# A decode step with attention and a feed-forward layer: the first piece of w2 is loaded as 112 rows, its last 16 rows by eight small transfers placed among wo's pieces

## The chip, the cores and the metric

The kernel runs on one core of a Trainium2 chip. The metric is the device time of one execution in microseconds (us); lower is better. Differences of about 0.2% (0.7 us) are what is looked at here.

## The reference

One token (batch 1, one query position, width 512) goes through a block whose layer norms are modulated by a condition `c`. Attention has 32 query heads on 8 key/value heads of size 128, over a cache of 32768 positions; the feed-forward layer is 512 to 1792 to 512 with a ReLU. All inputs are bfloat16.

```python
mod = silu(c) @ w_mod                      # six vectors of 512: sa, ca, ga, sb, cb, gb
h = layernorm(x) * (1 + ca) + sa
q = h @ wq                                 # 32 heads of 128
p = softmax(q @ k_cache.T * 128**-0.5)     # 4 query heads share one of 8 kv heads
x = x + ga * ((p @ v_cache) @ wo)          # wo: 4096 x 512
h = layernorm(x) * (1 + cb) + sb
x = x + gb * (relu(h @ w1) @ w2)           # w1: 512 x 1792, w2: 1792 x 512
```

The two caches are 64 MB each, so nearly all of the time is the reading of about 149 MB from HBM.

## The kernel before

**One stream of loads.** Everything large is loaded by SP (the SyncE queue) through one helper, `stream_dma` (line 141), in the order of the list `stream`: a half of K of head 0, `w_mod`, `wq`, the rest of K of head 0, then K of head g+1 and V of head g in turn, at the end V of the last head in three pieces, then the four pieces of `wo` (`WOP`: 4, 2, 1 and 1 kv heads, that is 2048, 1024, 512 and 512 KB), the two pieces of `w1` (`W1P`: 1344 and 448 KB) and the six pieces of `w2` (`W2P`: 512, 384, 384, 256, 128 and 128 KB). `need(key)` issues the list up to the key that is wanted; `load(key)` works out the tile and the source of one entry. Every one of these transfers has 128 rows, one for each partition of SBUF.

**Where they go.** Three slots of 64 KB per partition form a ring; `wo`, `w1` and `w2` share one slot, the tile `tail_sb`. The first transfer into it waits until the slot's earlier user, a K tile, has been read.

**Completion.** Each transfer adds to one of eight completion semaphores, taken in turn. A transfer that takes a semaphore waits, on SP, until the transfer eight before it has landed. For the last transfers of the list that means: `w1`'s second piece waits for the first V piece of the last head, `w2`'s first and second piece for the second and third; `w2`'s pieces three to six wait for `wo`'s four pieces.

**The end.** After the last head TensorE (PE) projects with `wo` (`project`, line 582 for the first three pieces, 588 for the last), VectorE (DVE) and ScalarE (ACT) do the second layer norm, PE does `w1` (line 744), the hidden row is transposed and put through the ReLU (lines 754 and 755), and PE works through `w2` piece by piece (line 767, four matmuls for each of 14 column blocks: 16, 12, 12, 8, 4 and 4 matmuls for the six pieces), each piece as soon as it has landed. Two DVE operations (lines 772 and 774) and the store of 1 KB (line 775) follow.

Of the kernel before, what the change touches and what calls it, by code (L numbers as in the profile page):

```python
# [17 lines left out]
def kernel(  # L18
# [28 lines left out]
    WOP = [(0, Hkv // 2), (Hkv // 2, Hkv // 4), (Hkv - 2, 1), (Hkv - 1, 1)]  # L47
    WOROWS = 3
    LAST = Hkv - 1
# [3 lines left out]
    W1P = [(0, KT - 1), (KT - 1, KT)]  # L53

    OUT0, OUT1 = 30, 34
    assert Dh == 128 and REP == 4 and D == 512 and FT == W2P[-1][1] and NTILE == 4
    scale = float(Dh) ** -0.5
    eps = 1e-5
# [8 lines left out]
    def wo_v(i):  # L67
        g0, n = WOP[i]
        return A_wo[g0 * REP * Dh:(g0 + n) * REP * Dh, :].rearrange("(p r) d -> p r d", p=P)
# [19 lines left out]
    loaded, last_loop, end_b = {}, [], []  # L89
# [12 lines left out]
    def piece(name, at, n):  # L102

        if name not in pieces:
            pieces[name] = ring.tile([P, NTILE * TK * Dh], BF16, tag="slot", name=name)
        return pieces[name][:, at:at + n]

    def load(key):
        kind = key[0]
        if kind == "wm":  # L110
            t = piece("wmq_sb", 0, WM).rearrange("p (kt n) -> p kt n", kt=KT)
            src = wm_v
        elif kind == "wq":
            t = piece("wmq_sb", WM, WQ).rearrange("p (kt n) -> p kt n", kt=KT)
            src = wq_v
        elif kind in "kv":
            g, steps = key[1], key[2]
            src = (kv if kind == "k" else vv)[g, :, TK * steps[0]:TK * (steps[-1] + 1), :]
            name = f"Ksb{g}" if kind == "k" else f"Vsb{g}"
            t = piece(name, TK * Dh * steps[0], TK * Dh * len(steps)).rearrange("p (j d) -> p j d", d=Dh)  # L120
        elif kind == "wo":
            g0, n = WOP[key[1]]
            t = piece("tail_sb", g0 * REP * D, n * REP * D).rearrange("p (r d) -> p r d", d=D)
            src = wo_v(key[1])
        elif kind == "w1":
            k0, k1 = W1P[key[1]]
            t = piece("tail_sb", WO + k0 * Dff, (k1 - k0) * Dff).rearrange("p (kt f) -> p kt f", f=Dff)
            src = w1_v[:, k0:k1]
        else:
            f0, f1 = W2P[key[1]]  # L130
            t = piece("tail_sb", WO + KT * Dff + f0 * D, (f1 - f0) * D).rearrange("p (f d) -> p f d", d=D)
            src = w2_v[:, f0:f1]
        stream_dma(t, src)
        if kind in "kv":
            for i, u in enumerate(steps):
                loaded[(kind, g, u)] = t[:, TK * i:TK * (i + 1), :]
        else:
            loaded[key] = t

    def stream_dma(dst, src):  # L140
        i = nc.sync.dma_start(out=dst, in_=src)  # L141
        tc.stamp_issue_order_token(i.ins, "sp_stream")
        if last_loop:

            tc.add_manual_dep(i.ins, last_loop[0], mybir.DependencyInfo(
                mybir.DependencyClass.NoSync, mybir.DependencyReason.DATA))

    whole, halves = [(0, 1, 2, 3)], [(0, 1), (2, 3)]
    stream = [("k", 0, halves[0]), ("wm",), ("wq",), ("k", 0, halves[1])]
    for g in range(LOOPED):  # L150
        stream += [("k", g + 1, s) for s in (halves if g >= HALVED else whole)] + [("v", g, s) for s in (halves if g >= HALVED else whole)]
    for s in halves:
        stream += [("k", LAST, s), ("v", LOOPED, s)]
    stream += [("v", LAST, (0, 1)), ("v", LAST, (2,)), ("v", LAST, (3,))] + [("wo", i) for i in range(len(WOP))]
    stream += [("w1", i) for i in range(len(W1P))] + [("w2", i) for i in range(len(W2P))]
    pos = [0]

    def need(key):
        while key not in loaded:
            load(stream[pos[0]])  # L160
            pos[0] += 1
        return loaded[key]
# [19 lines left out]
    for hp in range(4):  # L182
        h, par = hp // 2, hp % 2
        src = AP(ib.tensor, ib.offset + 64 * h + par, [[ib.ap[0][0], P], [0, 4], [2, 32]])
# [130 lines left out]
    for u in range(2):  # L315
        for half in range(2):
            t = need(("k", 0, u))[:, 32 * half:32 * half + 32, :].rearrange("p j d -> p (j d)").bitcast(F32)
# [488 lines left out]
```

## Time and profile before

| what | value |
|---|---|
| median of 3 runs | 354.75 us (354.69 to 354.9) |
| the profiled execution | 354.43 us |
| its span, from the first to the last instruction | 352.5 us |
| HBM read | 149.42 MB, 424 GB/s over the span |
| PE busy | 276.4 us (78%) |
| DVE busy | 200.9 us (57%) |

The profiled execution takes 1.93 us more than its span. Busy shares say little here: the 16 DMA engines are busy nearly all the time, and which wait ends last in the final 15 us is what an edit of the last loads touches. In a row of the windows view stand the window, its length, the busy time of each engine with its instructions, the granted TensorE clock, the mean busy share of the 16 DMA engines and the GB/s that they moved.

### The profile page before, as it was taken

The numbers are of one execution on the slowest core, as the hardware profiler recorded it, in microseconds if no ns is written. First come the engines' busy times: TensorE is split into PE (matmuls) and PEld (weight loads), VectorE is DVE, ScalarE is ACT, GpSimd is POOL, SyncE is SP. The second block draws the span as 40 slices with busy tenths as digits, with TensorE's granted clock in tenths as the row PEclk, the third lists the DMA queues.
The fourth block names the chain that finished last, engine by engine and source line by source line (L and its number), as shares of the span: only waits on it lengthen the run. The fifth ranks groups of instructions, "written<-read, shape, count | busy, mean of one in ns | idle before, by whom it ended". The sixth has DMA issues, their size and how long they took to land. (4 is left out here: it accounts for less than half of the span.)

```text
span 352.5 us, 3650 instructions
## 1 busy us (share of the span) xinstructions
PE 276.4 (78%) x1285; PEld 112.7 (32%) x1285; DVE 200.9 (57%) x226; ACT 25.1 (7%) x69; POOL 3.1 (1%) x15
## 2 busy tenths in 40 slices
PE   0055891995998599976998499867999789989976
PEld 0021330341333233422433233322444334434433
DVE  6662464984079613974099506975684357744142
ACT  1200103002000200001000200011000100011000
POOL 2000000000000000000000000000000000000000
PEclk9996897698999969996999989996999999999986
DMA  8999989989999999899899899999999999999995
GB/s 353 404 436 440 496 372 469 461 379 469 431 409 455 424 424 461 387 448 469 387 454 469 387 455 461 396 402 450 435 422 424 450 429 420 433 454 403 429 413 217
DMA packets 5379, 149.58 MB, mean 424 GB/s; under 512 B 632, under 2 KB 888, under 8 KB 1784
## 3 DMA queue, kind: packets, MB, share of 16 engines
q1 hardware_dynamic: 5336, 149.43, 98.5%
q8 instruction: 8, 0.13, 0.1%
q14 instruction: 3, 0.02, 0.0%
q10 hardware_dynamic: 32, 0.00, 0.0%
HBM read 149.42 MB, written 0.00 MB: 424 GB/s over the span
## 5 line engine op out<-in xcount | busy, mean ns | idle before, releaser
L426 DVE STREAM_TRANSPOSE Ksb<-Ksb 128x2048 f32<-128x2048 f32 x60 | 133.1, 2275 | 59.6 <-DMA Ksb<-in_A_k_cache_dram 59.6
L507 PE MATMUL o_ps<-Vsb,P_g 128*16 (+1 forms) x512 | 126.6, 405 | 13.3 <-ACT P_g L482 10.0
L445 PE MATMUL S_ps<-Ksb,qbd 128*128 128x512 bf16 x512 | 120.8, 388 | 10.4 <-DVE Ksb L426 8.7
L445 PEld LDWEIGHTS <-qbd 128*128 128x128 bf16 x512 | 49.8, 99 | 77.7 <-issue 21.8
L507 PEld LDWEIGHTS o_ps<-Vsb,P_g 128*16 x352 | 33.6, 95 | 68.2 <-issue 38.3
L507 PEld LDWEIGHTS <-P_g 128*16 128x16 bf16 x160 | 13.8, 90 | 19.0 <-issue 0.4
L407 ACT COPY qbd<-qrep_sb 32x16 bf16<-32x16 bf16 x32 | 6.4, 201 | 175.2 <-PE S_ps L445 174.0
L487 DVE STREAM_TRANSPOSE P_g<-P_g 128x1024 bf16<-128x1024 bf16 x8 | 10.0, 1245 | 14.1 <-ACT P_g L482 14.1
L458 DVE TENSOR_REDUCE m_p<-S_ps 128x1 f32<-128x1024 f32 x7 | 8.6, 1223 | 12.7 <-PE S_ps L445 12.7
L309 PE MATMUL mod_ps<-wmq_sb,siluT 128*1 128x512 bf16 x24 | 3.6, 623 | 9.9 <-DMA wmq_sb<-in_w_mod_dram 9.9
L318 DVE STREAM_TRANSPOSE Ksb<-Ksb 128x2048 f32<-128x2048 f32 x4 | 8.9, 2280 | 1.7 <-DMA Ksb<-in_A_k_cache_dram 1.7
L463 PE MATMUL mT_ps<-ident_f,m_p 128*1 128x128 f32 x8 | 2.2, 270 | 8.9 <-DVE m_p L458 7.9
L482 ACT ACTIVATE P_g<-S_ps,nbias 128x1024 bf16<-128x1024 f32 x8 | 8.9, 1114 | 0.2
L493 PE MATMUL L_ps<-Lexp,ones_f 128*128 128x4 f32 x16 | 3.1, 263 | 6.4 <-DVE Lexp L490 4.3
L496 DVE RECIPROCAL Linv<-L_ps 128x4 f32<-128x4 f32 x8 | 1.3, 164 | 11.7 <-PE L_ps L493 11.7
L479 ACT ACTIVATE nbias<-Mb_ps 128x1 f32<-128x1 f32 x8 | 1.4, 171 | 88.1 <-PE Mb_ps L477 88.1
L542 PE MATMUL acc_ps<-mask_sb,Y 16*128 16x4 f32 x16 | 3.1, 258 | 5.5 <-DVE Y L538 5.5
L239 PE MATMUL xc_ps<-cx_sel,wmq_sb 16*128 16x2 bf16 x4 | 0.3, 172 | 8.8 <-DVE wmq_sb L233 8.8
L535 DVE TENSOR_TENSOR o_ps<-o_ps,smask 16x512 f32<-16x512 f32 x8 | 5.3, 668 | 2.8 <-PE o_ps L507 2.8
L573 DVE CAST o_sb<-o_ps 128x4 bf16<-128x4 f32 (+2 forms) x4 | 0.7, 166 | 9.9 <-PE o_ps L569 9.9
L493 PEld LDWEIGHTS L_ps<-Lexp,ones_f 128*128 128x128 f32 x16 | 2.6, 203 | 9.7 <-issue 6.4
L538 DVE TENSOR_REDUCE Y<-o_ps 16x128 f32<-16x512 f32 x8 | 5.4, 679 | 0.3
(116 smaller groups left out, 80.6 us busy)
## 6 DMA issues: line engine op xcount, KB each, us to landing
Ksb<-in_A_k_cache_dram SPq DMA_DIRECT2D x6, 4096.0 KB, 30.3
Vsb<-in_A_v_cache_dram SPq DMA_DIRECT2D x5, 4096.0 KB, 29.5
wmq_sb<-in_A_wq_dram SPq DMA_DIRECT2D x1, 4096.0 KB, 28.1
Vsb<-in_A_v_cache_dram SPq DMA_DIRECT2D x2, 2048.0 KB, 35.5
wmq_sb<-in_w_mod_dram SPq DMA_DIRECT2D x1, 3072.0 KB, 18.9
tail_sb<-in_A_wo_dram SPq DMA_DIRECT2D x1, 2048.0 KB, 22.7
tail_sb<-in_B_w_dram SPq DMA_DIRECT2D x1, 1344.0 KB
tail_sb<-in_A_wo_dram SPq DMA_DIRECT2D x1, 1024.0 KB, 24.8
```

The costliest lines, as they stand in the source:

```text
L309: nc.tensor.matmul(dst[j // 4][32 * (j % 4):32 * (j % 4) + 1, :], lhsT=src_T[:, kt:kt + 1], rhs=w[:, kt, j * 512:(j + 1) * 512], start=(kt ...
L318: nc.vector.transpose(out=t, in_=t)
L407: nc.scalar.copy(out=o, in_=i)
L426: t = nc.vector.transpose(out=KTt.bitcast(F32), in_=KTt.bitcast(F32))
L445: nc.tensor.matmul(S_ps_tiles[g], lhsT=qbd[g % 2][:, hp, 4 * (7 - s):4 * (7 - s) + P], rhs=KTv[:, 16 * sl:16 * sl + 16, h, :, par], start= ...
L458: behind_loop(nc.vector.reduce_max(out=m_p[:], in_=S_g.rearrange("p g f -> p (g f)"), axis=AX.X))
L482: nc.scalar.activation(out=P_g[:], in_=S_g.rearrange("p g f -> p (g f)"), func=ACT.Exp, bias=nbias[:], scale=scale, accum_out=l_g[:],)
L487: behind_loop(nc.vector.transpose(out=P_g[:], in_=P_g[:]))
L493: nc.tensor.matmul(L_ps[:], lhsT=ones_f[:], rhs=Lexp[:], start=True, stop=True)
L507: nc.tensor.matmul(o_tiles[g][:], lhsT=PT, rhs=Vx, start=False, stop=False, skip_group_check=True)
L535: nc.vector.tensor_tensor(out=o, in0=o, in1=smask[:].unsqueeze(2).to_broadcast([16, 4, Dh]), op=ALU.mult,)
L538: nc.vector.tensor_reduce(out=Y[:], in_=o.rearrange("p s d -> p d s"), op=ALU.add, axis=AX.X)
```

## The change

The first piece of `w2` (key `("w2", 0)`) is loaded with 112 rows instead of 128. Its last 16 rows, 4 KB each, are loaded by eight transfers of 3, 1, 3, 1, 3, 1, 3 and 1 rows (`FEW`), and two of these stand in the list `stream` right behind each of the four pieces of `wo`, so ahead of `w1`. The bytes are the same, and so is the computation.

```diff
+    FEW = [((112, 115), (115, 116)), ((116, 119), (119, 120)), ((120, 123), (123, 124)), ((124, 127), (127, 128))]
...
             src = w2_v[:, f0:f1]
+            if len(key) > 2:
+                a, b = key[2:]
+                stream_dma(t[a:b], src[a:b])
+                return
+            if key[1] == 0:
+                a = FEW[0][0][0]
+                stream_dma(t[0:a], src[0:a])
+                loaded[key] = t
+                return
         stream_dma(t, src)
...
-    stream += [("v", LAST, (0, 1)), ("v", LAST, (2,)), ("v", LAST, (3,))] + [("wo", i) for i in range(len(WOP))]
+    stream += [("v", LAST, (0, 1)), ("v", LAST, (2,)), ("v", LAST, (3,))]
+    for i in range(len(WOP)):
+        stream += [("wo", i)] + [("w2", 0, a, b) for a, b in FEW[i]]
     stream += [("w1", i) for i in range(len(W1P))] + [("w2", i) for i in range(len(W2P))]
```

In the order of instructions that results, SP has 46 transfers instead of 38, and the eight completion semaphores go round over the longer list. Call the small transfers s1 to s8. Each waits, as every transfer does, for the one eight places ahead of it: s4 for the first V piece of the last head, `wo`'s third piece for the second V piece, s5 for the third, s6 for `wo`'s first piece, `wo`'s fourth for s1, s7 for s2, s8 for `wo`'s second piece, `w1`'s pieces for s3 and s4, and `w2`'s six pieces for `wo`'s third piece, s5, s6, `wo`'s fourth piece, s7 and s8. SP issues in order, so `wo`'s fourth piece stands behind s6's wait and `w1`'s first piece behind s8's. PE has the same matmuls in the same order and two more waiting instructions ahead of the first matmul of line 767, which now waits for five transfers' semaphores instead of one's.

## The prediction

> **What bounds the kernel now.** I read the page first, then the chain of waits, then the windows of the last 15 us.
>
> ```profile
> span 352.5 us, 3650 instructions
> DMA  8999989989999999899899899999999999999995
> q1 hardware_dynamic: 5336, 149.43, 98.5%
> q10 hardware_dynamic: 32, 0.00, 0.0%
> ```
>
> The third row is SP's queue: its packets take 98.5% of the time of 16 DMA engines. The kernel is a stream of loads, and an edit counts where it moves the end of that stream. The chain of waits that ended last (start, length, what):
>
> ```profile
> 313.44 24.82 DMA tail_sb<-in_A_wo_dram
> 338.25 0.02 issue
> 338.27 10.57 DMA tail_sb<-in_B_w_dram
> 348.84 0.04 issue
> 348.88 0.62 PE end_ps L767 x12
> 349.50 0.03 issue
> 349.54 0.29 PE end_ps L767 x4
> 349.83 0.03 issue
> 349.86 0.29 DVE o_rows L772
> 350.15 0.02 issue
> 350.17 0.28 DVE o_bf L774
> ```
>
> `wo`'s second piece lands at 338.25; at 338.27 SP may issue `w2`'s fourth piece, which lands at 348.84, and PE starts on it at 348.88. So the last link is the landing of `w2`, and what follows it (PE, two DVE operations, the store) is 352.5 - 348.84 = 3.7 us that the change doesn't touch. Now the windows (window, length, four engines with instructions, POOL, clock, DMA share, GB/s):
>
> ```profile
> 345.00:346.00 1.00, 1.00 (x16) 0.15 (x8) 0.00 (x0) 0.00 (x0) 0.00 (x0) 0.50 1.02 412
> 347.00:347.40 0.40, 0.35 (x8) 0.36 (x10) 0.00 (x0) 0.23 (x1) 0.00 (x0) 0.50 1.09 415
> 347.40:347.90 0.50, 0.50 (x16) 0.50 (x12) 0.00 (x0) 0.00 (x0) 0.00 (x0) 0.58 0.71 268
> 347.90:348.30 0.40, 0.40 (x20) 0.40 (x16) 0.00 (x0) 0.00 (x0) 0.00 (x0) 1.00 0.58 220
> 348.30:348.90 0.60, 0.42 (x16) 0.30 (x13) 0.00 (x0) 0.00 (x0) 0.00 (x0) 1.00 0.66 217
> 348.90:349.20 0.30, 0.30 (x8) 0.25 (x8) 0.00 (x0) 0.00 (x0) 0.00 (x0) 1.00 0.31 106
> 349.20:350.00 0.80, 0.58 (x12) 0.25 (x7) 0.14 (x1) 0.00 (x0) 0.00 (x0) 1.00 0.00 0
> ```
>
> Two things are to be seen. First, the 16 DMA engines don't end together: until 347.4 all are busy, by 347.9 to 348.3 about nine (0.58 x 16), and the last end at 349.2. Some lead the others by up to 349.2 - 347.4 = 1.8 us, and the laggards set the end. That is what this change can act on. Second, the engines that are left don't go faster: 220 GB/s over 9.3 engines are 23.7 GB/s each, with small rows, against 412/16 = 25.8 before. So a laggard isn't held by a common pool that the others drain; its limit is its own lane. Whether that lane is the engine, or the part of SBUF that it writes, these rows can't say: in the kernel before every large transfer has 128 rows, and I take it that each engine then has its own eight. This is the hinge of the forecast.
>
> **What the 112 rows save.** A row of 4 KB takes one engine 4096 / 25.8 GB/s = 0.16 us (row 345 to 346). If 112 rows are 16 x 7, each engine has one row less: the laggards end 0.16 us sooner, at 349.04, and with them the three last landings, PE and the end. That is all there is to win: 0.04%.
>
> **What the small transfers add.** Sixteen rows of 4 KB go elsewhere. The fourth row of the first fence shows how few rows are dealt out: its 32 packets are the two loads of `c` and `x`, 8 rows each, so 8 packets of data and 8 of completion for each load, one row an engine. By that, 3 rows use three engines and 1 row one. If they are the same three and one each time, one engine gets 4 x 2 = 8 rows and two get 4: net +7 x 0.16 = 1.1 us and +3 x 0.16 = 0.5 us. Leaders with 1.8 us in hand swallow this. The Trainium skill (DMA: Bandwidth & Descriptors, "Why a DMA increments its semaphore by 16 and not by 1") says that a transfer runs on the largest number up to 16 that divides the slowest dimension larger than one, on the lowest-numbered engines. For loads of 8 rows the 32 packets agree. For the single row, 2048 elements long, the rule would give 16 pieces of 256 B instead of one engine; with the four single rows on everyone, 1 KB or 0.04 us each, the saving would be 0.12 us instead of 0.16.
>
> **What they cost where they land.** The 16 rows are partitions 112 to 127, and each group of partitions is then written by an engine that in all other transfers writes elsewhere; the 112-row piece, cut in sevens, is out of step with the eights of the others too. If the lane is the engine, this is free. If the lane is the part of SBUF, two engines meet in one lane and each gets half. I work this out for a laggard. (a) Each lane of partitions 112 to 127 takes in 4 foreign rows while its own engine is busy with `wo`: 4 x 0.16 = 0.64 us. (b) The 7 rows of the laggard's own share of `w2`'s first piece meet another engine's: 14 x 0.16 = 2.24 us instead of 8 x 0.16 = 1.28, so +0.96. (c) Leaders, with 0.7 us of lead left (SP's queue, below), come to their 112-row share while laggards are still in `w1`'s second piece; two of those four rows in a laggard's lane cost 0.32. Sum +1.9 us. From below the bound is the free case, -0.16. From above, three engines in one lane in (b): 21 x 0.16 = 3.4 instead of 1.28, +2.1, with (a) +2.7. No row of the trace shows two engines in one lane; nearest are the rows above, in which a lone engine keeps to 24 to 26 GB/s with seven or more neighbours gone, as it would if its place in SBUF were the limit and as it need not if that place had room. I take +1.9, the case of two.
>
> The Trainium skill (SBUF — State Buffer, "Door 1: The DMA port swizzle") speaks against the change at this place: bandwidth depends on how many of 16 ports the partitions reach, one port takes about 27 GB/s, and its table has 16 partitions at 104 GB/s, a quarter of the whole. By its formula the three rows of each small transfer lie in one port. No transfer of this trace tests it; the 25.8 GB/s an engine only stay below its figure.
>
> **SP's queue.** Eight issues are added, and the waits for a completion semaphore move.
>
> ```profile
> SPq L141 <- DMA Vsb<-in_A_v_cache_dram: 15.1, 3, 6.0
> SPq L141 <- DMA tail_sb<-in_A_wo_dram: 8.3, 4, 4.3
> 0.74 0.41 SPq L141 DMA_DIRECT2D Ksb<-in_A_k_cache_dram  x1
> 1.21 0.41 SPq L141 DMA_DIRECT2D wmq_sb<-in_w_mod_dram  x1
> 335.81 5.26 SPq L141 DMA_DIRECT2D tail_sb<-in_B_w_dram  x4
> 1.20:1.70 0.50, 0.00 (x0) 0.00 (x0) 0.32 (x2) 0.02 (x1) 0.50 (x3) 1.00 0.00 0
> 1.70:2.20 0.50, 0.00 (x0) 0.00 (x0) 0.50 (x3) 0.50 (x1) 0.50 (x3) 1.00 3.46 985
> ```
>
> Above: SP's waits (total us, times, longest), its issues, and the windows of the start. In the kernel before only pieces of `w1` and `w2` stand behind these seven waits, issued 8 to 20 us ahead of their data. Afterwards `wo`'s fourth piece comes behind the landing of `wo`'s first (335.81, the fifth row) and `w1`'s first piece behind that of the second (338.25). One issue goes with the next every 0.47 us (0.74 to 1.21). The first load was issued at 0.74 and no data flowed before 1.7: 1.0 us. So `w1` is issued at 338.25 + 0.47 = 338.72 and flows at 339.7. What do the engines have until then? The last issue in the fifth row waits for `wo`'s fourth piece and ends at 341.07, so it began at 340.7: `wo` lands then for the laggards, whose data end some 0.3 before (349.2 against a last landing of 349.5), at 340.4. They have 0.7 us in hand and don't run dry. Leaders run dry at 340.4 - 1.8 = 338.6 and stand for 1.1 us: their lead shrinks from 1.8 to 0.7. I cost this at nothing for the end; its cover is these 0.7 us. If `w1`'s first data took more than 1.7 us from its issue, everything behind would be late by what goes over.
>
> **PE.** Two more waiting instructions:
>
> ```profile
> L767 PEldq EVENT_SEMAPHORE  x1: 51/51/51, 346.3 to 346.3; - x1
> 347.05 1.66 PE L767 MATMUL end_ps<-tail_sb 128*32 128x128 bf16 x40 [0.30 <-ACT tail_sb L755]
> ```
>
> One took 51 ns at 346.3, and the matmuls wait for ACT until 347.05: 0.1 us under a cover of 0.7. Nothing is removed from PE, DVE or ACT.
>
> **The sum.** Span 352.5 + 1.9 = 354.4; with 1.93 around it 356.33, against 354.43 for the profiled execution; that one lies 0.32 under the median, so 356.6 us by the median. 0.2% (0.7 us) is about what a measurement of this kernel can tell from no change.
>
> **The rivals.**
> 1. Lanes are the engines: no collision, every laggard saves a row, 354.75 - 0.16 = 354.6. For it: the dealing of rows puts the extra ones on few engines, and leaders exist. Against: it needs those engines to be leaders, and nothing shared where they write. Not slower. Chance 0.25.
> 2. The engine that gets eight rows is a laggard: no collisions, but the end moves by 7 x 0.16 = 1.1 us, to 355.9. It decides when that engine's lead is under 1.1 us. The windows show that about half of the engines are laggards, but not which. Chance 0.08.
> 3. SP's waits starve the stream: if first data take over 1.7 us from the issue, laggards run dry. Each us beyond that is one us; 2.7 us instead of 1.0 would give 355.75. Against: the 1.0 us of the start. Chance 0.08.
> 4. Evening out: the leaders' stop lets the rest go faster or brings all ends together. The rows from 347.4 hold 0.71 x 0.5 + 0.58 x 0.4 + 0.66 x 0.6 + 0.31 x 0.3 = 1.08 us of all 16, so a perfect balance would end at 348.48, 0.72 sooner: 354.0. One row an engine can't bring that. Chance 0.04.
>
> **How the numbers follow.** Collisions have 0.55: 356.6, own range from 355.4 (only (a)) to 357.45 (three in a lane). Slower by over 0.2%: collisions 0.55, rivals 2 and 3 0.16, together 0.71. Within 0.2%: rival 1, 0.25. Faster by over 0.2%: 0.04. The range has to take in rival 1, because without it more than two in ten would be left out: from 354.5 to 357.5.
>
> **What would show it.** If collisions are right, the windows of the end show a DMA share of 1 or more with fewer GB/s while the 112 rows flow, `w2`'s fourth piece lands 1 to 3 us later than 348.84, and `wo`'s first piece, which SP's sixth small transfer waits for, lands some 0.6 after 335.8. If rival 1 is right, the share stays near full until 348.5 and falls at once, and `w2`'s fourth piece lands at 348.7. If rival 2 is, the last stretch has a share of about 0.06 (one engine of 16) for a microsecond. If rival 3 is, a stretch around 340 has a share well under 0.5. A `w1` that flows before 339 would make the step on SP wrong; an end before 354.5 or after 357.5 the whole.

## The result and the profile after

The changed kernel takes 356.72 us (median of 6 runs, 356.34 to 357.1) against 354.82 us before: a ratio of 1.0053, with a 95% interval from 1.004 to 1.0066. It is slower by 1.9 us (0.53%). In a later comparison (e10, below) the ratio was 1.0055 (1.0038 to 1.0071). The profiled execution took 357.08 us, its span is 355.3 us. Differences in us here and below are worked out from the recorded ratios, which can lie up to 0.7 us off the difference of two medians (e4).

The first lines of the page and its SP queue:

```profile
span 355.3 us, 3660 instructions
q1 hardware_dynamic: 5352, 149.43, 98.4%
```

The queue has 16 packets more than before (5352 against 5336). Eight transfers of 3 and 1 rows on three engines and one give 16 packets of data and 16 of completion, and the 112-row piece has 16 rows less: +16. So a single row did go to one engine. The rule of the Trainium skill that the prediction weighed (DMA: Bandwidth & Descriptors, "Why a DMA increments its semaphore by 16 and not by 1"), read for a row of 2048 elements, would have given 16 pieces and 16 completions for each, +136 packets. What fails is that reading and not the rule: the trace has the single row as an instruction of one element of 4096 B, and for a pattern of size 1 the Trainium skill too has one engine.

The windows of the changed kernel's end (window, length, PE, PE's weight loads, DVE, ACT, POOL, clock, DMA share, GB/s):

```profile
337.00:339.00 2.00, 0.91 (x18) 0.47 (x10) 1.22 (x4) 0.00 (x0) 0.00 (x0) 1.00 1.01 367
339.00:341.00 2.00, 1.06 (x14) 0.28 (x6) 0.46 (x2) 0.00 (x0) 0.00 (x0) 1.00 1.02 304
...
345.00:346.00 1.00, 0.28 (x5) 0.13 (x8) 0.61 (x4) 0.00 (x0) 0.00 (x0) 0.50 1.03 352
346.00:347.00 1.00, 1.00 (x12) 0.27 (x5) 0.00 (x0) 0.00 (x0) 0.00 (x0) 0.50 1.04 251
347.00:347.40 0.40, 0.07 (x4) 0.00 (x0) 0.00 (x0) 0.00 (x0) 0.00 (x0) 0.50 1.14 307
347.40:347.90 0.50, 0.45 (x4) 0.09 (x3) 0.00 (x0) 0.00 (x0) 0.00 (x0) 0.50 0.97 205
...
349.20:350.00 0.80, 0.68 (x14) 0.71 (x16) 0.00 (x0) 0.00 (x0) 0.00 (x0) 0.50 1.04 401
...
350.50:351.00 0.50, 0.50 (x12) 0.36 (x8) 0.00 (x0) 0.00 (x0) 0.00 (x0) 0.50 0.49 176
...
351.50:352.00 0.50, 0.50 (x16) 0.50 (x12) 0.00 (x0) 0.00 (x0) 0.00 (x0) 0.50 0.07 25
```

From 346 to 348 the engines are busy all the time (share about 1) and move 205 to 307 GB/s, where the kernel before moved 412 with the same share. This is where the 112 rows flow: packets that take longer, not engines that stand. The data end at about 352 instead of 349.2. A first loss lies earlier, from 337 to 341 (367 and 304 GB/s), where the kernel before moved:

```profile
337.00:339.00 2.00, 1.31 (x14) 0.58 (x12) 1.22 (x4) 0.00 (x0) 0.00 (x0) 1.00 1.02 419
339.00:341.00 2.00, 0.88 (x15) 0.40 (x14) 0.88 (x2) 0.00 (x0) 0.00 (x0) 1.00 1.04 438
```

The same stretches by PE's matmuls: start, length, line, tile, and in brackets the idle time before with its releaser. First the kernel before, then the changed one:

```profile
338.30 0.60 PE L582 MATMUL end_ps<-tail_sb,o_sb 128*1 128x512 bf16 x8
339.54 0.39 PE L582 MATMUL end_ps<-tail_sb,o_sb 128*1 128x512 bf16 x4 [0.29 <-DMA tail_sb<-in_A_wo_dram]
344.55 1.66 PE L744 MATMUL hid_ps<-tail_sb,h2T 128*1 128x448 bf16 x16 [0.27 <-DVE h2T L292]
```

```profile
338.72 0.60 PE L595 MATMUL end_ps<-tail_sb,o_sb 128*1 128x512 bf16 x8 [0.48 <-DMA tail_sb<-in_A_wo_dram]
340.26 0.39 PE L595 MATMUL end_ps<-tail_sb,o_sb 128*1 128x512 bf16 x4 [0.59 <-DMA tail_sb<-in_A_wo_dram]
345.78 1.29 PE L757 MATMUL hid_ps<-tail_sb,h2T 128*1 128x448 bf16 x12 [0.72 <-DVE end_ps L750]
347.45 0.54 PE L757 MATMUL hid_ps<-tail_sb,h2T 128*1 128x448 bf16 x4 [0.37 <-DMA tail_sb<-in_B_w_dram]
349.32 3.29 PE L780 MATMUL end_ps<-tail_sb 128*32 128x128 bf16 x56 [0.80 <-ACT tail_sb L768]
```

`wo`'s second piece is used 0.4 us later than before, its third 0.7 us later; the second piece of `w1`, which PE never waited for, now holds it until 347.45; and `w2` begins at 349.32 instead of 347.05. That last row names ACT, which was done by 349.03. What came last was `w2`'s first piece: the trace also records when each engine completed its share of a transfer, and the last engine was done with that piece at 349.23 (346.29 before). The end of the changed kernel's chain of waits:

```profile
348.54 0.23 ACT tail_sb L768
348.77 0.01 issue
348.79 0.24 ACT tail_sb L768
349.03 0.29 issue
349.32 3.30 PE end_ps L780 x56
352.63 0.02 issue
352.65 0.29 DVE o_rows L785
352.94 0.02 issue
352.97 0.28 DVE o_bf L787
```

PE now runs through all 56 matmuls without a stop, in 3.30 us, 59 ns each, at a granted clock of 0.50 (the windows above); before, 40 took 1.66 us (41 ns each), the clock came back to 1.00 at 347.9, and PE stood waiting for `w2`. So in the changed kernel the late start of `w2` and the late end of the data (the last engine completes at 352.19, 349.50 before) lead to nearly the same end.

Of the signs that were named: the share stays near 1 with fewer GB/s; `w2`'s fourth piece is complete at 351.55, 2.7 us later; `wo`'s first piece at 336.17, 0.4 us later and not 0.6. No stretch around 340 has a share under 0.5.

### The profile page after: what moved, and what is told of

Same layout as the page of the kernel before. It is cut to its first block, busy times and chain, and to the rows that moved or that the text cites. A ratio compares the mean times of both kernels' runs of the same rounds, so it can differ in the third digit from the quotient of the medians.

```text
span 355.3 us, 3660 instructions
## 1 busy us (share of the span) xinstructions
PE 277.3 (78%) x1285; PEld 113.5 (32%) x1285; DVE 200.9 (57%) x226; ACT 25.1 (7%) x69; POOL 3.1 (1%) x15
## 3 DMA queue, kind: packets, MB, share of 16 engines
q1 hardware_dynamic: 5352, 149.43, 98.4%
```

## The experiments

Three theories: **collisions** (a lane is the part of SBUF that is written; rows that are out of step meet there), **engines** (lanes are the DMA engines; only their shares of rows count) and **SP's waits** (the completion semaphores hold `w1` back and the stream runs dry). The lines of `stream` and `load` are those of the change unless a diff says otherwise.

**e1. Half of the partitions at a time.**

```diff
+            if key[1] == 0:                      # w1's first piece, on the kernel before
+                stream_dma(t[0:64], src[0:64])
+                stream_dma(t[64:128], src[64:128])
...
```

> The kernel before, with w1's first piece (1344 KB) loaded as two transfers of 64 rows, rows 0 to 63 and then 64 to 127. Bytes, order and engines' shares stay (four rows of 10.5 KB for each of 16 engines, twice). Collisions (the lane is the part of SBUF that is written): if the lanes go by groups of partitions, each half reaches only some of them, and two engines share each lane: with half of the lanes 8 rows x 0.40 us = 3.2 us become 6.4, so +2 to +3.2 us. Lanes are the engines: no change, within 0.2 us. SP's waits: one more transfer far from the end of the queue, no change.

Measured: 1.0147 (1.0125 to 1.017), +5.2 us. Its windows:

```profile
340.00:341.00 1.00, 0.39 (x4) 0.09 (x3) 0.00 (x0) 0.00 (x0) 0.00 (x0) 1.00 0.96 197
341.00:343.00 2.00, 0.57 (x9) 0.25 (x9) 0.72 (x1) 0.00 (x0) 0.00 (x0) 0.83 1.07 240
343.00:345.00 2.00, 1.63 (x20) 1.12 (x20) 0.78 (x7) 0.00 (x0) 0.00 (x0) 0.50 1.00 263
...
347.00:348.00 1.00, 0.00 (x0) 0.00 (x0) 0.00 (x0) 0.00 (x0) 0.00 (x0) 0.50 0.92 206
...
349.00:350.00 1.00, 1.00 (x12) 0.44 (x16) 0.00 (x0) 0.00 (x0) 0.00 (x0) 0.50 1.02 415
```

All 16 engines are busy and move about half of what they do with 128 rows. The engine isn't the lane: the same engines with the same shares slow down by about half when the rows lie in 64 partitions (a packet of `w1`'s first piece takes 0.75 us in the median, 0.40 before). The low rate lasts some 8 us. It sets in at 340 with the leaders' rows of `w1`, while laggards are still in `wo`'s fourth piece, whose last engine completes at 343.11 (340.73 before); the +3.2 us that I had allowed counted `w1`'s own rows alone. The Trainium skill (SBUF — State Buffer, "Door 1: The DMA port swizzle") has 196 GB/s for 64 partitions; the 197 to 263 of these windows, in which other rows flow too, are near it.

**e2. The 112 rows without the small transfers.**

```diff
+            if key[1] == 0:                      # w2's first piece, on the kernel before
+                stream_dma(t[0:112], src[0:112])
+                stream_dma(t[112:128], src[112:128])
...
```

> The kernel before, with w2's first piece loaded as 112 rows and, right behind, one transfer of its last 16 rows. No small transfers among wo's pieces. Collisions: the 112 rows out of step cost (b) and (c), +1.3 us, and the 16 rows, four to a lane, 0.3 to 0.6 more: +1 to +1.9 us. Lanes are the engines: each engine has 7 + 1 rows again, no change. SP's waits: no change, since nothing is put ahead of wo's and w1's issues.

Measured: 1.006 (1.0043 to 1.0077), +2.1 us. The rows in question:

```profile
343.00:345.00 2.00, 1.56 (x12) 0.48 (x16) 1.26 (x7) 0.29 (x1) 0.00 (x0) 0.50 1.05 299
345.00:346.00 1.00, 0.88 (x12) 0.18 (x5) 0.00 (x0) 0.00 (x0) 0.00 (x0) 0.50 1.00 261
346.00:347.00 1.00, 0.51 (x5) 0.12 (x4) 0.00 (x0) 0.00 (x0) 0.00 (x0) 0.50 1.06 237
```

Share 1, GB/s down to 237: the changed kernel's picture, with nothing put among `wo`'s pieces. It begins before 345, when the laggards are still in `w1` (eight engines complete its second piece only from 345.59 on): part (c). Splitting a transfer of 128 rows into 112 and 16 costs 2 us with every engine's number of rows unchanged.

**e3. The small transfers with a full first piece.**

```diff
-            if key[1] == 0:                      # the changed kernel
-                a = FEW[0][0][0]
-                stream_dma(t[0:a], src[0:a])
-                loaded[key] = t
-                return
```

> The changed kernel, but w2's first piece is loaded in full (128 rows); the eight small transfers stay, so their 16 rows are loaded twice and w2's first piece waits on SP for the last small ones. Collisions: only part (a), +0.64 us against the kernel before. Lanes are the engines: no change, or +0.1. SP's waits starve the stream: everything that the changed kernel lost by the landing of w1's first piece, +1.0 to +1.7 us.

Measured: 1.0043 (1.0025 to 1.0061), +1.5 us. That is more than (a) alone: SP's waits cost something.

**e4 and e8. Eight transfers that move next to nothing.**

```diff
+        if kind == "x":                          # on the kernel before; x stands where the small transfers stand
+            a, b = key[1:]
+            stream_dma(extra[a:b], w2_v[a:b, 0, 0:P])
+            return
...
```

> The kernel before with eight more transfers in the places of the small ones, of 3 and 1 rows, but of 256 B a row into a spare tile; w2's first piece has 128 rows. The completion semaphores and SP's waits are those of the changed kernel; next to nothing is moved and nothing is missing from w2. Collisions: no change (16 rows of 256 B are 0.01 us each). Lanes are the engines: no change. SP's waits starve the stream: the laggards run dry before w1's first data, +0.5 to +1.0 us.

> The eight transfers of 256 B a row once more, in five rounds, because the first interval was wide (1.0012 to 1.0069). SP's waits starve the stream: +0.5 to +2 us, with a scatter of about 1 us from run to run, since it hangs on which engines run dry. Collisions and lanes that are engines: no change.

Measured: 1.004 (1.0012 to 1.0069) and in the repetition 1.0039 (1.0023 to 1.0056), +1.4 us, with runs from 355.14 to 357.86. This I had costed at nothing. SP's issues and two windows of e4:

```profile
336.50 2.02 SPq L148 DMA_DIRECT2D extra<-in_B_w_dram  x2
338.57 5.41 SPq L148 DMA_DIRECT2D tail_sb<-in_B_w_dram  x8
```

```profile
340.00:340.50 0.50, 0.00 (x0) 0.00 (x0) 0.49 (x1) 0.00 (x0) 0.00 (x0) 1.00 0.72 249
340.50:341.00 0.50, 0.22 (x9) 0.21 (x10) 0.22 (x1) 0.00 (x0) 0.00 (x0) 1.00 0.60 237
```

`w1`'s first piece is issued at 338.57, as worked out (338.7), but between 340 and 341 the engines' share is 0.6 to 0.7 at 240 GB/s, where the kernel before moved:

```profile
340.00:341.00 1.00, 0.25 (x9) 0.23 (x10) 0.69 (x1) 0.00 (x0) 0.00 (x0) 1.00 1.04 440
```

So 1.4 to 2.4 us after its issue `w1` still didn't flow on all engines. I had 1.0 us from the first load of the kernel and 0.7 us of cover. The packets in e4's trace show which part of that was wrong. The first of `w1` begin at 339.55, 1.0 us after the issue, as I had it; but twelve of the first 16 then take 0.46 to 1.66 us, where each one in the kernel before takes 0.40. The engines come late by different amounts: 13 complete their share of `w1`'s first piece by 344.54, the other three at 345.52, 345.92 and 346.31.

**e5. Four transfers instead of eight.**

```diff
-    FEW = [((112, 115), (115, 116)), ((116, 119), (119, 120)), ((120, 123), (123, 124)), ((124, 127), (127, 128))]
+    FEW = [((112, 115),), ((116, 119),), ((120, 123),), ((124, 127),)]      # on e4
```

> The kernel before with four more transfers of 256 B a row (3 rows each, into a spare tile), one behind each of wo's pieces, instead of eight. w1's first piece then waits for the landing of wo's first piece (335.8) instead of its second (338.3), 2.4 us earlier, and nothing but that differs from the eight. SP's waits starve the stream: the stop goes, and with it the loss: no change against the kernel before, within 0.2 us. If instead small transfers as such disturb the stream, half of the loss of the eight stays, +0.7 to +1.0 us.

Measured: 1.0006 (0.9997 to 1.0015): no loss. `w1` is issued 2.4 us earlier:

```profile
336.13 5.75 SPq L148 DMA_DIRECT2D tail_sb<-in_B_w_dram  x8
```

So the loss of e4 comes with the wait for a completion semaphore: four small transfers that don't lengthen that wait cost nothing.

**e6 and e12. Small rows by themselves, without that wait.** Two transfers of 8 rows (e6), or five of 3, 3, 3, 3 and 4 rows (e12), with all 128 rows of the first piece.

```diff
+    FEW = [((112, 120),), ((120, 128),), (), ()]                                         # e6
+    FEW = [((112, 115), (115, 118)), ((118, 121),), ((121, 124),), ((124, 128),)]        # e12
```

> The kernel before with two more transfers of 8 rows of 4 KB, partitions 112 to 119 behind wo's first piece and 120 to 127 behind its second; w2's first piece has all 128 rows, so these 16 rows are loaded twice. w1's pieces wait for V pieces that landed long before, so SP's waits starve nothing. Collisions: part (a) by itself, four foreign rows in a lane, +0.64 us, seen from the landing of wo's first or second piece on. Lanes are the engines: within 0.2 us (two more rows on eight engines; 0.3 us if one of them is a laggard).

> The same five transfers, but w2's first piece with all 128 rows (16 rows are loaded twice; that piece waits on SP for the small ones). Collisions: (a) by itself, +0.6 to +0.8 us as with the two transfers of 8 rows. Lanes are the engines: within 0.2 us.

Measured: e6 1.0023 (1.0012 to 1.0034), +0.8 us; e12 1.0016 (1.0005 to 1.0026), +0.6 us. Part (a) had 0.64.

**e7 and e11. The change without SP's wait.** The same two lists, with the 112-row piece.

> The change without its starving: w2's first piece as 112 rows, its last 16 by two transfers of 8 rows, behind wo's first and second piece. Collisions: (a), (b) and (c), +1.9 us, and what the trace of the 112 rows alone showed, +2.2. If collisions were slight and the changed kernel's loss were SP's waits, within 0.3 us of the kernel before.

> The changed kernel with its last 16 rows in five transfers of 3, 3, 3, 3 and 4 rows instead of eight, so that w1's first piece waits for the first of them (landed by about 336) and not for wo's second piece: the changed kernel without its starving, and with the same three engines for nearly all small rows. If the small rows on leading engines, the 112 rows and SP's waits each cost what they cost alone, +1.5 to +2.8 us by (a) to (c) and none by the waits. If the waits are the whole of the changed kernel's loss, within 0.3 us of the kernel before. If the waits' stop lessens the collisions, this is slower than the changed kernel, +2.5 us or more.

Measured: e7 1.0078 (1.0063 to 1.0093), +2.8 us; e11 1.0058 (1.0041 to 1.0076), +2.1 us. e11 is the changed kernel with `w1` issued in time (and with five small transfers for eight), and it loses as much as the changed kernel. Its windows show the low rate where the 112 rows flow, and none before:

```profile
337.00:339.00 2.00, 0.92 (x18) 0.43 (x10) 1.01 (x3) 0.00 (x0) 0.00 (x0) 1.00 1.03 398
339.00:341.00 2.00, 1.27 (x14) 0.32 (x13) 0.54 (x2) 0.00 (x0) 0.00 (x0) 1.00 1.06 427
...
344.00:345.00 1.00, 0.73 (x3) 0.20 (x2) 0.74 (x5) 0.29 (x1) 0.00 (x0) 0.50 1.06 251
345.00:346.00 1.00, 0.76 (x12) 0.32 (x13) 0.30 (x2) 0.00 (x0) 0.00 (x0) 0.50 1.05 248
346.00:347.00 1.00, 0.56 (x12) 0.10 (x4) 0.00 (x0) 0.00 (x0) 0.00 (x0) 0.50 1.00 248
347.00:348.00 1.00, 1.00 (x5) 0.16 (x4) 0.43 (x2) 0.00 (x0) 0.00 (x0) 0.50 1.03 236
```

**e9 and e10. Do the losses add?** e9 is e4 with e2's edit; e10 is the changed kernel again.

> Both halves of the loss without the 4 KB rows among wo's pieces: the eight transfers of 256 B a row (SP's waits as in the changed kernel, +1.4 us alone) and w2's first piece as 112 rows and one transfer of 16 rows (+2.2 us alone). If the two losses add, +3.6 us. If the stop that SP's waits make brings the leaders back to the laggards, so that fewer rows meet in a lane, the sum is smaller, +1.9 to +2.6 us, near the changed kernel's own loss.

> The changed kernel once more, on the chip of the run above: +1.9 us against the kernel before, below the +2.8 us that the 112 rows and two transfers of 8 rows cost without SP's waits.

Measured: e9 1.0102 (1.0054 to 1.0149), +3.6 us, from 1.9 to 5.3; e10 1.0055 (1.0038 to 1.0071). e9's value is that of a sum, but its interval holds both theories: inconclusive. No version beat the kernel before.

**The same by stages.** The traces let the losses be told apart by place. A stage here is the time between two completions, each that of the last of the 16 engines: from the second V piece of the last head to `wo`'s fourth piece, from there to `w1`'s first piece, and from there to `w2`'s first piece. The first row is in us, the others are the change against it, one traced execution each:

| kernel | to `wo`'s fourth | to `w1`'s first | to `w2`'s first |
|---|---|---|---|
| before | 14.63 | 3.22 | 2.35 |
| 16 small rows, 128-row piece (e6, e12) | +0.66, +0.61 | -0.03, -0.03 | -0.04, -0.06 |
| 112 and 16 rows (e2) | -0.01 | +0.43 | +1.35 |
| 16 small rows, 112-row piece (e7, e11) | +0.78, +0.69 | +0.54, +0.49 | +1.31, +1.37 |
| the wait alone (e4, e8) | 0.00, -0.01 | +2.35, +1.07 | +0.04, +0.04 |
| the wait, 16 small rows, 128-row piece (e3) | +0.63 | +2.47 | +0.04 |
| the wait, 112 and 16 rows (e9) | 0.00 | +3.84 | +1.36 |
| the changed kernel (first run, e10) | +0.67, +0.59 | +1.02, +0.80 | +1.24, +1.30 |

The small rows cost 0.6 to 0.8 us in the first stage wherever they stand, the 112 rows 1.2 to 1.4 us in the third, and the wait 0.8 to 3.8 us in the second. So each of the three has a loss of its own. The sums are of single executions: the two of the changed kernel took 357.08 and 357.09 us, the one of the kernel before 354.43.

## Why the prediction was right, and where it wasn't

**The number.** 356.6 was forecast, 356.72 measured. The sum was collisions alone, +1.9 us; e11, which has the collisions and not the wait, measures +2.1 us (1.5 to 2.7).

**The hinge.** Whether the lane is the engine or the place was my choice, with 0.55 for the place. e1 decides it: same engines, same shares, half the partitions, about half the rate. In every run here row p of a weight goes to partition p, so the place in SBUF and the place of the source in HBM change together; the figure cited at e1 speaks for SBUF, but no run here separates the two.

**(a) 0.64 us.** Two kernels with this part alone: +0.6 (0.2 to 0.9) and +0.8 us (0.4 to 1.2). In the changed kernel `wo`'s second and third piece are used 0.4 and 0.7 us later, and the first stage is longer by 0.59 to 0.78 us in every kernel with the 16 small rows, by nothing in the others of the table.

**(b) and (c), 1.28 us together.** In the changed kernel the third stage is longer by 1.24 and 1.30 us. Without the wait it is more: e11 less e12 is 2.1 - 0.6 = 1.5 us, e7 less e6 2.8 - 0.8 = 2.0 us, and some 0.5 us of it falls into the second stage. That fits (c), which counts leaders' rows in laggards' lanes: with the wait the first engine completes `w1`'s first piece at 343.97, in e11 at 342.48, so without the wait the leaders are further ahead. The packets show the sharing by rows: in the kernel before each 4 KB row of `w2`'s first piece takes 0.16 us; in the changed kernel the 112 rows take 0.16 to 0.34, 0.22 on average (e11 0.25). The two in a lane of the forecast would be 0.32 for every row, so rows share their lane for part of their time, and the 3 KB rows of the next two pieces share too (0.17 instead of 0.12), which I hadn't counted. Which rows meet in which lane isn't in the traces.

**The saving of 0.16 us** can't be seen: in no kernel did the 112 rows gain anything. e2 gives each engine eight rows as before and so leaves it out; it costs as much as the others.

**SP's waits, costed at nothing.** This step failed. The issue at 338.7 was about right (338.57 in e4, 338.96 in the changed kernel), and so was the 1.0 us until the first data; that the engines then run at full rate was not. Most first packets after the stop are longer, by up to 1.3 us in e4. The kernel before showed as much at its start: the packets that begin at 1.77 to 2.16 take 1.62 to 2.13 us, later ones of the same size mostly 1.21 to 1.23, which the window that I read from 1.70 on doesn't show. Alone the wait costs 1.4 us (e4, e8), rival 3 in kind, though I gave it 0.08. In the changed kernel it adds nothing that the times can show: with the wait 1.0053 and 1.0055, without it (e11) 1.0058. The stages show a part of the reason: the wait costs 0.8 to 1.0 us in the second, where e11 loses 0.5 us already because its leaders are ahead, so the difference is only 0.3 to 0.5 us. Why the second stage lost 2.3 to 3.8 us in the traces of e3, e4 and e9, where two or three engines come far behind the rest, and only 0.8 to 1.0 in the two of the changed kernel, is open. So the total, right to 0.1 us, is in part luck: a real loss was left out, and the time doesn't show it.

**What follows the landing.** I wrote that the 3.7 us behind the landing of `w2`'s fourth piece aren't touched. In the changed kernel the last chain is another: `w2` begins late, and PE at a clock of 0.50 needs 3.30 us for it without a stop, nearly as long as the data.

**The rivals.** Rival 1 (no collisions) falls with e1 and e2. Rival 2 (the engine with eight rows is a laggard) falls with e4's trace: the three engines of the small transfer behind `wo`'s fourth piece complete it at 339.45, 339.48 and 340.01, the one of the single row behind it at 339.63, and that piece's eight laggards are done only from 340.54 on. Besides, e2, in which no engine has more rows than before, loses as much.

## What to carry to other kernels

In this stream, transfers of all 128 partitions kept the 16 engines out of each other's way; 112, 64 or a few rows didn't, and a stream at full rate paid for that though the bytes stayed the same. Handing rows over evened out nothing here, since what is full is the place of the rows and not the engine. And before small transfers are put into a queue, count the completion semaphores: each one more pulls the wait of a later, large transfer nearer, and four were free here where eight cost 1.4 us. When a total comes out right, look whether its terms did: here the stages between completions told the three losses apart, and one of them had been left out.

## What had not been expected of the hardware

After the stream had run thin, data came back 1.0 us after the issue, but slowly: in e4 the engines moved about 240 GB/s between 340 and 341, and the loss of e4 and e8 scattered from 0.3 to 3 us between runs (355.14 to 357.86 against 354.8). And splitting one transfer of 1.4 MB into halves of 64 partitions slowed what flowed ahead of it too, `wo`'s fourth piece by 1.8 us in the first stage, because the engines aren't at the same transfer at the same time.
